# A planned attention and FFN kernel: chunk bounds in another PSUM bank, DMA lateness in the planner, and a refit plan

## The chip, the cores and the metric

The kernel runs on one core of a Trainium2 chip. The metric is device time in microseconds (us) of one execution. The kernel before takes 265.7 us, the median of 13 runs.

## The reference

Four sequences (`B` = 4) of 768 tokens with 8 heads of 64 go through block-sparse causal attention, and its output through a feed-forward network (FFN).

```python
k_min, k_max = k_chunks.min(3), k_chunks.max(3)           # 24 chunks of 32 keys
ub = sum_d(maximum(q * k_min, q * k_max))                 # bound per query and chunk
top_chunks = argsort(where(causal_chunk, ub, -1e9))[..., -6:]
scores = where(in top_chunks and causal, q @ k.T / 8, -1e9)
x = softmax(scores) @ v                                   # [3072, 512]
out = relu(x @ w_in) ** 2 @ w_out                         # 512 -> 2048 -> 512
```

Inputs and output are f32; the kernel computes in bf16 with f32 sums.

## The kernel before

**The work.** A sequence is cut into 6 query tiles of 128. The first tile sees at most four chunks, so its attention needs no selection: it runs densely for all sequences at the start (`first_transposes`, `first_attention`), and the resulting 4 x 128 tokens are the first batch of FFN rows. For the other five tiles the heads go in pairs, 16 in all (`p` = 0 to 15, four to a sequence), in two steps.

`stage_a(p)` prepares a pair. It has the keys and queries with the head dimension on partitions: for sequences 0 and 1 TensorE transposes them into PSUM (`kT`, `qT`); for sequences 2 and 3 (`b >= BY_DMA`, with `BY_DMA` = 2) SP's DMA transposes put them into SBUF (`kt`, `qt`). VectorE then takes chunk maxima and minima (`kr`, L681, two reductions of 0.94 us a pair), spreads them into `kbd`, splits the queries into positive and negative parts (`qp`, `qm`), and copies keys and queries into the operands of the scores (`kqc`, `qsc`). TensorE multiplies to the bounds `ub`, 128 x 240 f32 in PSUM. VectorE adds the causal mask (`ubm`, L706), takes the eight largest of each row (`m`, L655, ten instructions), and compares with the sixth (`selb`). The selection is transposed to `sT`, on TensorE for sequences 0 and 1, by SP's DMA transpose for 2 and 3, and copied into `qsc` as 24 more contraction rows, so that the score matmul itself adds a large negative number to chunks not selected.

`stage_b(p, x)` runs ten banks of scores for a pair (`ps`, L766), ScalarE's exponential (`e`, L788), the causal mask on the diagonal tiles (VectorE L743 or GpSimd L746), the value products (`av`, L777), and VectorE's division into `x` (L594, L596).

`ffn` turns a sequence's `x` into `xT` (TensorE transposes, or SP's DMA transposes for sequences 1 and 2), multiplies by `w_in` (`up`, `ph`, L850), applies ReLU on ScalarE or VectorE (`ht`, L857 and L859), squares on VectorE (`h`, L868), multiplies by `w_out` (`down`, `py`, L881), copies to `ob` and stores a row tile by SP. FFN matmuls are TensorE's filler while VectorE prepares the next pairs.

**The order.** Each operation is recorded with the engines that may do it and a cost on each, a due time, and the tiles it touches. `Plan.order` plays the whole kernel once in the planner's own time. At each step it looks for what can start first, and among the operations of that engine that can start within `wait` of it takes the one with the smallest due time. A load by GpSimd may start only in the order of the string `loads`, then of `later`. The result, sorted by planned start, is written out under a manual schedule, so every engine's instruction order is fixed. `Transfers` is the planner's picture of the DMA engines: it says when a load or transpose ends. Waits on the chip are by semaphores, whatever the planner thought. The numbers in `P` set the due times: `lead` is how far ahead of its scores a pair is prepared, `f_due` places the first tiles, `up_due` and `up_rate` the first FFN batch, `due` and `rate` the other four, `va`, `vm`, `ra`, `h2` the small operations in a pair or FFN step.

**The PSUM banks.** Eight: `tp` 1, `ps` 3, `av` 2, `ff` 2. `kT` and `qT` use `tp`. `ub` and the scores share the three `ps` banks. For sequences 2 and 3 nothing but the DMA transposes takes the place of `kT` and `qT`, so `tp` has no user there.

**The SBUF buffers that the order turns on.** `nt` has 6 for loads that wait for their DMA transpose (the `sT` of sequences 2 and 3 uses the same tag), `kq` 6, `ob` 3, `e` 6.

Of the kernel before, what the change touches and what calls it, by code (L numbers as in the profile page):

```python
# [9 lines left out]
F32 = mybir.dt.float32  # L10
# [31 lines left out]
class Transfers:  # L42
# [10 lines left out]
    def run(self, queues, until):  # L53
        now = self.now
        while now < until and any(queues.values()):
            active = [q for q in queues.values() if q]
            rate = self.RATE / len(active)
            span = min([until - now] + [q[0][1] / rate for q in active])
            now += span
            for q in active:  # L60
                q[0][1] -= span * rate
                if q[0][1] < 1e-6:
                    op = q.pop(0)[0]
                    op.end = now + (0.85 if op.turns else 0.35)
        return until if until < 1e8 else now

    def add(self, op):
# [10 lines left out]
class Plan:  # L78
# [17 lines left out]
        self.ops = []  # L96
        self.loads = []

    def op(self, where, due, fn, needs=(), tiles=(), packets=0, turns=False):
        op = Op(where, due, fn, [n for n in needs if n is not None],  # L100
                [t for t in tiles if t is not None], packets, turns)
        for t in op.tiles:
            t.users.append(op)
        op.number = -1 if packets and not turns else len(self.ops) - len(self.loads)
        self.ops.append(op)
        if packets and not turns:
            self.loads.append(op)
        return op
# [92 lines left out]
def kernel(  # L201
# [11 lines left out]
    B, H, S, D = q.shape  # L213
    CH = 32
    NC = S // CH
# [9 lines left out]
    NP = H // 2  # L225


    NS = NT - 1
    QC = 128 * NS
    VW = 80  # L230
    NSET = 4
    P = dict(lead=[38, 70, 77, 66, 65, 20, 16, 23, 34, 24, 32, 68, 19, 63, 66, 67],
             f_due=[-89, -30, -320.97, -400.97], sp='K0 Q0 K1 Q1', rows=-379,
             rows_after=0, up_due=-1.28, up_rate=3.88, half=4, due=[-6, 1, 3, 45],
             rate=[3.07, 2.84, 4.48, 1.87], va=13.9, vm=5.92, ra=2.68, h2=-1.11,
             later='k1 q1 v1 q2 k2 q3 v3 v2 k3', shift={}, p0=-5650, wait=0.01,
             loads="k0 Q3 K3 q0 Q2 K2 V0 V3 V2 V1 v1 "
                   "k1 i0 v0 i3 q1 i2 v2 k2 i1 q2 o0 q3 k3 o1 o2 v3 o3")

    nc.scalar.preload_act_table_set("natural_log_exp_and_others")  # L240

# [105 lines left out]
    order = []  # L347

    def load(key, fn, due, packets, tiles=(), cost=0.88):
        op = plan.op({"POOL": cost}, due, fn, tiles=tiles, packets=packets)  # L350
        loaded.setdefault(key, []).append(op)

    def first_of(nm, b):
# [12 lines left out]
    BY_DMA = 2  # L366
    turned = {}
    for b in range(B):
        for nm in "kq":
            if b < BY_DMA:  # L370
                nat[nm, b] = buffer("kq", [128, NS, H, D], name=nm + "n")
            else:
                turned[nm, b] = buffer("kq", [128, NT if nm == "k" else NS, NP, 128],
                                       name=nm + "t")

    def turn_by_dma(dst, src, due, needs, tiles, packets=1270):
        return plan.op({"SP": 1.2}, due, lambda _: nc.sync.dma_start_transpose(
            out=dst(), in_=src()), needs, tiles, packets=packets, turns=True)

    raws = {}  # L380

# [33 lines left out]
    def load_turned(nm, b, j, due):  # L415
        dst = turned[nm, b]
        if j == 0:
            src, needs = None, loaded[nm, b, "first"] + loaded[nm, b, 1]
        else:
            src = buffer("nt", [128, H, D])  # L420
            load((nm, b, j), lambda _: nc.gpsimd.dma_start(
                out=src.tile,
                in_=SRC[nm][b, :, 128 * j:128 * (j + 1)].rearrange("h p d -> p h d")),
                due, 1024, [src])
            needs = loaded[nm, b, j]
        i = j if nm == "k" else j - 1
        op = turn_by_dma(
            lambda: dst[:, i],
            lambda: (src.tile if src else firsts[nm][:, b]).rearrange(
                "p h d -> p (h d)"), due, needs, [src, dst])  # L430
        loaded.setdefault((nm, b), []).append(op)

    def load_tile(nm, b, j, due):
# [44 lines left out]
    for what in P["loads"].split():  # L478
        i = int(what[1])
# [10 lines left out]
    for what in P["later"].split():  # L490
        nm, b = what[0], int(what[1])
# [121 lines left out]
    def stage_a(p):  # L613
        b, hp = divmod(p, NP)
# [7 lines left out]
            qT = buffer("tp" if p else "ps", [128, QC], name="qT")  # L622
        kr = buffer("kr", [128, 2, NC])
        qp, qm = buffer("qp", [128, QC]), buffer("qm", [128, QC])
        ub = buffer("ps", [128, NS, 2, NC], F32, name="ub")
        ubm = buffer("ubm", [128, NS, 2, NC], F32)
        m8 = buffer("m8", [128, NS, 2, 8], F32)
        sT = buffer("nt" if b >= BY_DMA else "ps", [128, NT // 2, 128], name="sT")
# [39 lines left out]
        late = 4 if p == 0 else 0  # L668
        if b >= BY_DMA:
            got = list(loaded["k", b])  # L670
            kc_on, qc_on, q_on = {"DVE": 0.36}, {"DVE": 0.40}, 0.39
        else:
            got = [op({"PE": 0.34}, t0, turn_keys, loads_of("k", b, hp) + [made["ident"]],
                      [kT, nat["k", b]])]
            kc_on, qc_on = {"DVE": 0.475, "ACT": 0.74}, {"ACT": 0.63, "DVE": 0.41}
            q_on = 0.40
# [130 lines left out]
    def ffn(x, ready, rows, by_dma, due, rate, up_tags=("ff", "ff")):  # L807
# [12 lines left out]
        def turn(t):  # L820
            if by_dma:
                xt_made.append(turn_by_dma(
                    lambda: xT[:, t], lambda: x[:, t], step(0.225), ready(t),
                    [xT] + xs))
                return
            pt = buffer("ff", [128, NKI, 128], name="xt")

            def go(_):
                for ki in range(NKI):
                    transpose(pt[:, ki], x[:, t, 128 * ki:128 * (ki + 1)])  # L830

# [6 lines left out]
        h2 = {}  # L838

        def up(f, c0, c1, i):  # L840
            tag = up_tags[i % 2]
            w = c1 - c0
            ph = buffer(tag, [128, w], F32, name="ph")
            ht = buffer("ht", [128, w])
            if f not in h2:
                h2[f] = buffer("h2", [128, 128 * n])

            def go(_):
                for ki in range(NKI):
                    nc.tensor.matmul(  # L850
                        ph.tile, lhsT=w_in_sb[:, ki, 128 * f:128 * (f + 1)],
                        rhs=xT[:, c0 // 128:c1 // 128, ki],
                        start=(ki == 0), stop=(ki == NKI - 1))
# [67 lines left out]
    for b in range(B):  # L921
        x = buffer("x", [128, NS, d_model])
        x_done[b, 1] = []
        for p in range(NP * b, NP * (b + 1)):
            stage_a(p)
            stage_b(p, x)
        last = b == B - 1
        turn, up, down = ffn(
            x, lambda t, b=b: x_done[b, 1], [S * b + 128 * t for t in range(1, NT)],
            0 < b < B - 1, HALVES * NP * (b + 1) + P["due"][b], P["rate"][b], ("ps", "ps") if last else ("ff", "ff"))  # L930
        for c in range(2):
            tiles = range(2 * c, 2 + (NS - 2) * c)
            for t in tiles:
                turn(t)
            for f in range(NFI):
                up(f, 128 * tiles[0], 128 * (tiles[-1] + 1), f)
        for t in range(NS - last):
            down(t)
        if last:
            down(NS - 1, 0, 384)  # L940
            down(NS - 1, 384)
# [35 lines left out]
```

## Time and profile before

| What | Value |
|---|---|
| median of 13 runs (lowest to highest) | 265.7 us (264.56 to 266.93) |
| the profiled execution | 265.2 us, span 263.4 us |
| busy: TensorE, VectorE, ScalarE, GpSimd | 252.1, 195.5, 181.8, 104.9 us |
| `ph` and `py` matmuls (L850, L881), busy | 97.1 and 92.5 us |
| DMA: loads by GpSimd's queue | 13.11 MB in 75088 packets |
| median time from issue to landing: `kt`, `qt`, `xT`, `sT` | 3.1 (`kt` from `nt`), 4.8, 2.8, 2.4 us |
| mean granted TensorE clock | 0.994 |

The span runs from the first to the last instruction; 1.8 us of the execution's time lie around it. The slices of the page show the loads filling the DMA engines for about the first half, GpSimd busy with issuing them in the same time, VectorE near full until some 150 us, and TensorE near full from 20 us to the end. Matmuls are pipelined and their ends are modelled, so TensorE's busy share says less than the spacing of its starts.

### The profile page before, as it was taken

What the parts mean: (1) busy time and instruction counts of PE and PEld (TensorE: products, weight loads), DVE (VectorE), ACT (ScalarE), POOL (GpSimd) and SP (SyncE); (2) the same over time, 40 slices, a digit from 0 to 9 for tenths busy, and PEclk for the clock granted to TensorE, in tenths of its full rate; (3) what the DMA queues carried; (4) which work ended last, traced back from release to release, by engine and by line L of the source; (5) the groups of instructions that cost most, each with busy time, mean ns of one, the idle gap of its engine ahead of it and who ended that gap; (6) DMA issues with size and microseconds to landing.
All of it is one profiled execution on the core that took longest, in us unless ns stands there. A gap on an engine that the chain in (4) does not pass through costs nothing.

```text
span 263.4 us, 6518 instructions
## 1 busy us (share of the span) xinstructions
PE 252.1 (96%) x2391; PEld 162.3 (62%) x2391; DVE 195.5 (74%) x687; ACT 181.8 (69%) x372; POOL 104.9 (40%) x182
## 2 busy tenths in 40 slices
PE   7779999999999999998899999999999999999995
PEld 2447655665787665565586665567876548565443
DVE  5699899969998999999999979856777503455000
ACT  1679697973699978795788976688998315276112
POOL 8998868698247697632121221120012000000000
PEclk9799999999999999999999999999999999999999
DMA  9999999999999999983630001335000021100222
GB/s 147 163 181 186 189 181 197 158 121 192 194 83 149 146 144 151 167 124 95 118 97 4 0 2 55 113 82 116 2 0 2 0 80 42 40 5 0 80 80 80
DMA packets 103808, 26.11 MB, mean 99 GB/s; under 512 B 96312, under 2 KB 100832, under 8 KB 103776
## 3 DMA queue, kind: packets, MB, share of 16 engines
q0 software_dynamic: 75088, 13.11, 67.0%
q1 hardware_dynamic: 28688, 12.59, 21.5%
q8 instruction: 18, 0.29, 0.5%
q14 instruction: 14, 0.11, 0.1%
HBM read 27.26 MB, written 6.29 MB: 127 GB/s over the span
## 4 chain that ended last, share of the span: by engine, by line
PE 67%; DVE 20%; ACT 6%; DMA 4%; issue 2%; SPq 1%; DVEq 0%; ACTq 0%
PE ph L850 25%; PE py L881 24%; PE ps L766 8%; DVE kr L681 5%; PE av L777 5%; ACT e L788 2%; DVE m L655 2%; DMA raw<-in_k_dram 2%; DVE h L868 2%; DVE qsc L273 2%; DVE kqc L273 2%; DMA xT<-x 2%; ACT ht L857 1%; ACT qsc L271 1%; DVE qm L697 1%
## 5 line engine op out<-in xcount | busy, mean ns | idle before, releaser
L788 ACT ACTIVATE e<-ps 128x512 bf16<-128x512 f32 x160 | 89.2, 608 | 12.9 <-PE av L777 6.6
L850 PE MATMUL ph<-xT,w_in_sb 128*128 128x256 bf16 (+2 forms) x592 | 97.1, 304 | 0.9 <-DMA xT<-x 0.6
L881 PE MATMUL py<-w_out_sb,h 128*128 128x512 bf16 (+2 forms) x400 | 92.5, 370 | 0.0
L850 PEld LDWEIGHTS <-w_in_sb 128*128 128x128 bf16 x592 | 55.7, 97 | 23.8 <-issue 1.1
L746 POOL TENSOR_SCALAR_AFFINE_SELECT e<-e 128x128 bf16<-128x128 bf16 (+1 forms) x88 | 30.2, 344 | 94.1 <-ACT e L788 90.7
L857 ACT ACTIVATE ht<-ph 128x256 bf16<-128x256 f32 (+2 forms) x121 | 54.6, 455 | 18.0 <-PE ph L850 14.3
L868 DVE TENSOR_TENSOR h<-ht 128x256 bf16<-128x256 bf16 (+2 forms) x148 | 47.2, 328 | 14.6 <-ACT ht L857 10.6
L766 PE MATMUL ps<-qsc,kqc 88*128 88x128 bf16 (+1 forms) x320 | 54.7, 272 | 2.2 <-DVE ubm L706 1.5
L881 PEld LDWEIGHTS <-h 128*128 128x128 bf16 x400 | 35.5, 97 | 31.3
L777 PEld LDWEIGHTS <-e 128*128 128x128 bf16 x640 | 35.1, 97 | 11.8 <-DVE e L743 0.3
L271 ACT COPY ob<-py 128x512 f32<-128x512 f32 (+2 forms) x23 | 13.1, 569 | 35.0 <-PE py L881 34.8
L777 PE MATMUL av<-vn,e 128*128 128x65 bf16 x480 | 35.6, 193 | 0.0
L766 PEld LDWEIGHTS <-kqc 88*128 88x128 bf16 x320 | 26.0, 97 | 12.8 <-issue 3.4
L271 ACT COPY qsc<-sT 24x384 bf16<-24x384 bf16 (+1 forms) x39 | 17.1, 439 | 3.7 <-PE sT L276 2.2
L596 DVE TENSOR_TENSOR x<-av,rc 128x320 bf16<-128x320 f32 (+1 forms) x40 | 18.9, 472 | 0.5
L655 DVE MAX8 m<-ubm 128x8 f32<-128x24 f32 x160 | 15.6, 172 | 0.2
L681 DVE TENSOR_REDUCE kr<-kT 128x24 bf16<-128x768 bf16 x16 | 14.9, 951 | 0.4 <-PE kT L276 0.3
L681 DVE TENSOR_REDUCE kr<-kt 128x24 bf16<-128x768 bf16 x16 | 15.1, 941 | 0.0
L859 DVE TENSOR_SCALAR ht<-ph 128x256 bf16<-128x256 f32 (+2 forms) x27 | 13.0, 486 | 2.4 <-PE ph L850 2.1
L743 DVE TENSOR_TENSOR e<-e,tri 128x128 bf16<-128x128 bf16 (+1 forms) x40 | 9.8, 248 | 6.7 <-ACT e L788 5.9
L777 PE MATMUL av<-v,e 128*128 128x65 bf16 x160 | 14.6, 193 | 0.0
L273 DVE COPY xT<-xt 128x512 bf16<-128x512 bf16 x10 | 4.1, 420 | 12.3 <-PE xt L276 12.3
(85 smaller groups left out, 247.8 us busy)
## 6 DMA issues: line engine op xcount, KB each, us to landing
out_dram<-ob SPq DMA_DIRECT2D x23, 256.0 KB, 2.4
w_in_sb<-in_moe_w_in_dram POOLq DMA_DIRECT2D x4, 512.0 KB, 7.7
w_out_sb<-in_moe_w_out_dram POOLq DMA_DIRECT2D x4, 512.0 KB, 8.0
vn<-in_v_dram POOLq DMA_DIRECT2D x15, 128.0 KB, 6.1
nt<-in_q_dram POOLq DMA_DIRECT2D x10, 128.0 KB, 5.1
nt<-in_k_dram POOLq DMA_DIRECT2D x10, 128.0 KB, 5.0
kn<-in_k_dram POOLq DMA_DIRECT2D x8, 80.0 KB, 6.0
qn<-in_q_dram POOLq DMA_DIRECT2D x8, 80.0 KB, 7.3
```

What stands on the lines that cost most here:

```text
L271: nc.scalar.copy(dst, src)
L596: return plan.op({"DVE": 0.06 + 0.00108 * D * n}, due, lambda _: nc.vector.tensor_mul(x(), av[:, :, 0:D], rc[:, 0:n].unsqueeze(2).to_broad ...
L655: nc.vector.max(out=m8[:, i, hh], in_=ubm[:, i, hh])
L681: nc.vector.tensor_reduce(kr[:, mm].rearrange("d (t c) -> d t c", c=128 // CH) if b >= BY_DMA else kr[:, mm], part(kT).rearrange("d t (c j ...
L746: nc.gpsimd.affine_select(out=e, in_=e, compare_op=ALU.is_ge, fill=0.0, base=0, channel_multiplier=-1, pattern=[[0, n], [1, 128]])
L766: nc.tensor.matmul(ps[:, 128 * c:128 * (c + nt)], lhsT=kqs[:, s, hh, 128 * j:128 * (j + 1)], rhs=qss[:, s, hh, 128 * (t0 - 1):128 * (t0 - ...
L777: nc.tensor.matmul(av[:, t - 1], lhsT=e[:, 128 * c:128 * (c + 1)], rhs=value_tile(b, h, j), start=(i == 0 and c == 0), stop=(i == len(BANK ...
L788: nc.scalar.activation(e.tile, ps.tile, ACT.Exp, scale=scale), [sc], [ps, e])
L850: nc.tensor.matmul(ph.tile, lhsT=w_in_sb[:, ki, 128 * f:128 * (f + 1)], rhs=xT[:, c0 // 128:c1 // 128, ki], start=(ki == 0), stop=(ki == N ...
L857: nc.scalar.activation(ht.tile, ph.tile, ACT.Relu)
L868: {"DVE": 0.067 + w / 1920}, at[0] + P["h2"], lambda _: nc.vector.tensor_mul(h2[f][:, c0:c1], ht.tile, ht.tile), [op], [ht, h2[f]])))
L881: nc.tensor.matmul(py.tile, lhsT=h2[f][:, 128 * t:128 * (t + 1)], rhs=w_out_sb[:, f, c0:c1], start=(f == 0), stop=(f == NFI - 1))
```

## The change

Three things change in the text. The bounds `ub` of sequences 2 and 3 are put into the `tp` bank instead of a `ps` bank. The planner's operations get a lateness, added to the time at which a transfer ends in `Transfers`: 0.5 us for loads, 6.0 us for the transposes of keys and queries, 2.0 us for those of `xT`, none for `sT`; three VectorE costs of sequences 2 and 3 are raised. And nearly all numbers of `P` are others, with another order of loads. No operation is added or taken away; a lateness is no instruction, it moves what the planner lets start after it. The kernel after has five more lines, so its line numbers are up to five higher.

```diff
-                    op.end = now + (0.85 if op.turns else 0.35)
+                    op.end = now + (0.85 if op.turns else 0.35) + op.late
...
-    P = dict(lead=[38, 70, 77, 66, 65, 20, 16, 23, 34, 24, 32, 68, 19, 63, 66, 67],
-             f_due=[-89, -30, -320.97, -400.97], sp='K0 Q0 K1 Q1', rows=-379,
-             rows_after=0, up_due=-1.28, up_rate=3.88, half=4, due=[-6, 1, 3, 45],
-             rate=[3.07, 2.84, 4.48, 1.87], va=13.9, vm=5.92, ra=2.68, h2=-1.11,
-             later='k1 q1 v1 q2 k2 q3 v3 v2 k3', shift={}, p0=-5650, wait=0.01,
-             loads="k0 Q3 K3 q0 Q2 K2 V0 V3 V2 V1 v1 "
-                   "k1 i0 v0 i3 q1 i2 v2 k2 i1 q2 o0 q3 k3 o1 o2 v3 o3")
+    P = dict(lead=[6, 6, 76, 53, 65, 39, 26, 47, 78, 40, 11, 72, 73, 39, 58, 38],
+             f_due=[-36, 144, -224.97, -459.97], sp='K0 Q0 K1 Q1', rows=-639,
+             rows_after=0, up_due=-0.28, up_rate=9.32, half=4, due=[4, -34, -6, 45],
+             rate=[2.94, 3.93, 4.84, 2.12], va=7.79, vm=16.73, ra=0.45, h2=-0.81,
+             later='k1 q1 v1 k2 q2 q3 v2 v3 k3', shift={}, p0=-4820, wait=0.01,
+             loads="q0 K2 V0 k0 Q3 K3 k1 V3 Q2 V2 V1 "
+                   "i0 v1 v0 q1 v2 i2 i3 q2 o0 k2 i1 v3 k3 q3 o3 o1 o2")
...
-        op = plan.op({"POOL": cost}, due, fn, tiles=tiles, packets=packets)
+        op = plan.op({"POOL": cost}, due, fn, tiles=tiles, packets=packets,
+                     late=0.5)
...
-                "p h d -> p (h d)"), due, needs, [src, dst])
+                "p h d -> p (h d)"), due, needs, [src, dst], late=6.0)
...
-        ub = buffer("ps", [128, NS, 2, NC], F32, name="ub")
+        ub = buffer("tp" if b >= BY_DMA else "ps", [128, NS, 2, NC], F32, name="ub")
...
-            kc_on, qc_on, q_on = {"DVE": 0.36}, {"DVE": 0.40}, 0.39
+            kc_on, qc_on, q_on = {"DVE": 0.45}, {"DVE": 0.45}, 0.42
...
-                    [xT] + xs))
+                    [xT] + xs, late=2.0))
...
-            tag = up_tags[i % 2]
+            tag = up_tags[i % len(up_tags)]
```

In `loads` a capital letter with a number is the first tile of a sequence's keys, queries or values; a small `k`, `q` or `v` with a number is that pair of heads of sequence 0, the other five tiles; `i` and `o` are quarters of `w_in` and `w_out`.

More of the change, by code (lines that the diff above doesn't have):

```diff
@@ L97, in __init__, with op @@
         self.loads = []
-    def op(self, where, due, fn, needs=(), tiles=(), packets=0, turns=False):
+    def op(self, where, due, fn, needs=(), tiles=(), packets=0, turns=False,
+           late=0.0):
         op = Op(where, due, fn, [n for n in needs if n is not None],
@@ L103, in op @@
             t.users.append(op)
+        op.late = late
         op.number = -1 if packets and not turns else len(self.ops) - len(self.loads)
@@ L374, with turn_by_dma @@
                                        name=nm + "t")
-    def turn_by_dma(dst, src, due, needs, tiles, packets=1270):
+    def turn_by_dma(dst, src, due, needs, tiles, packets=1270, late=0.0):
         return plan.op({"SP": 1.2}, due, lambda _: nc.sync.dma_start_transpose(
-            out=dst(), in_=src()), needs, tiles, packets=packets, turns=True)
+            out=dst(), in_=src()), needs, tiles, packets=packets, turns=True,
+            late=late)
     raws = {}
@@ L929 @@
             x, lambda t, b=b: x_done[b, 1], [S * b + 128 * t for t in range(1, NT)],
-            0 < b < B - 1, HALVES * NP * (b + 1) + P["due"][b], P["rate"][b], ("ps", "ps") if last else ("ff", "ff"))
+            0 < b < B - 1, HALVES * NP * (b + 1) + P["due"][b], P["rate"][b],
+            ("ps", "ps") if last else ("ff", "ff"))
         for c in range(2):
```

## The prediction

> **What bounds the kernel now.** First the page's busy line, then the table of busy times by stretch, then the waits and the chain inside the stretch that stands out.
>
> ```profile
> PE 252.1 (96%) x2391; PEld 162.3 (62%) x2391; DVE 195.5 (74%) x687; ACT 181.8 (69%) x372; POOL 104.9 (40%) x182
> ```
>
> TensorE looks 96% busy, but that share can't tell full speed from starved. So I count what it streams. In the chain, sixteen 128x512 matmuls take 3.45 us, 0.216 each; four of 384 columns 0.65, so 0.162; four of 256 columns 0.44, so 0.11; transposes stand 0.055 apart, the 65-column value products 0.031. Times their counts in the groups: `ph` 83, `py` 83, `ps` 35, `av` 21, transposes 11, the rest 7: **240 us of streaming in a 263.4 us span**. The other 23 us are what can be won. Setting each matmul's start against the streaming done before it ("lag" = time minus streamed work), I read from the trace: lag 13.0 us at 10 us of work, 13.1 at 25, 14.0 at 35, 14.6 at 50, 15.1 at 60, 15.8 at 80, 17.5 at 110, 19.6 at 130, 19.8 at 190, 20.1 at 240, and 3.2 us from the last matmul to the end. So 13 us go at the start, 2.1 between 10 and 60, **4.5 between 60 and 130**, almost nothing after.
>
> ```profile
> 23.00:38.00 15.00, 14.98 (x145) 9.91 (x145) 13.99 (x53) 11.69 (x24) 11.85 (x15) 1.00 1.65 187
> 38.00:60.00 22.00, 21.64 (x256) 14.28 (x255) 19.81 (x69) 18.53 (x37) 17.60 (x28) 1.00 1.74 163
> 60.00:83.00 23.00, 22.92 (x249) 16.75 (x246) 21.56 (x76) 15.76 (x35) 13.81 (x22) 1.00 1.67 150
> 83.00:125.00 42.00, 40.63 (x411) 25.34 (x410) 41.44 (x144) 34.71 (x70) 25.16 (x44) 1.00 1.66 139
> 125.00:152.00 27.00, 25.93 (x256) 18.42 (x255) 25.99 (x83) 22.77 (x52) 5.89 (x15) 1.00 0.25 53
> 152.00:207.00 55.00, 55.00 (x586) 37.02 (x585) 41.54 (x156) 44.21 (x90) 8.65 (x26) 1.00 0.18 45
> ```
>
> Columns: stretch, length, then PE, PEld, DVE, ACT, POOL busy, clock, DMA. From 83 to 125 us VectorE is busy 41.44 of 42: it is the bound there. From 152 on TensorE is.
>
> ```profile
> PE ps L766 <- DVE ubm L706: 1.5, 3, 0.7
> ACT qsc L271 <- PE sT L276: 1.3, 1, 1.3
> ```
>
> These are waits between 95 and 130 us. The first is the one the bank edit aims at: three score groups waited for a `ps` bank held by chunk bounds that a late VectorE had not read.
>
> ```profile
> 123.00 0.40 DVE x L596
> 123.40 0.86 DVE kr L681
> ...
> 125.56 4.41 DMA xT<-x
> 129.98 0.05 issue
> 130.03 1.06 PE ph L850 x8
> ```
>
> The same stretch's chain: sequence 1's last attention output (123.0), then its DMA transposes, then the FFN matmuls 7.0 us later. TensorE stood 0.74 us at that point.
>
> **The Trainium skill.** "Perfetto Trace Analysis", Identifying the Most-Contended Engine, says that matmul busy share is no measure of distance to the limit; here 40.63 of 42 us busy hides 3 us of lag. "TensorE: Matmul & The Clock Gate", Back-to-back issue gap, gives N/2.4+2.5 ns for an isolated matmul and 131 ns sustained at N=512; the trace shows 216, so the measured spacing is used. "DMA: Bandwidth & Descriptors", Issuing engines are not separate DMA queues, says that DMAs from different engines share the same 16 DMA engines; the trace agrees: `kt` transposes land 2.5 us after issue at 113 to 121 us, `qt` transposes 6.6 us at 93 to 99, beside ten `vn` loads. "PSUM — Partial Sum Buffer", Terms, has one matmul output in one bank; the planner too gives the small `ub` a whole one.
>
> **The change part by part.** The DMA lateness and the refit numbers change the order only. Counting both recorded orders, every VectorE, ScalarE and TensorE operation is there in both; some move between engines (8 selection copies from ACT to DVE, 3 query and 2 `xT` copies the other way, causal masks on DVE 40 to 38, and 20 small warm-up transposes for 2 large warm-up matmuls); the new expression for the tag of `ph` picks the same tag. VectorE's total is 178.4 us in both, by start-to-start spacings where it never waits (kr 0.86, max 0.084, qp and qm 0.395, qsc 0.45 to 0.48, kqc 0.37 or 0.48, x 0.40, h 0.20 to 0.33, and so on). Against its busy time up to 152 us (140.1) that sum (132.7) is low by a factor 1.056, used below. What differs is **how much VectorE work stands ahead of how much TensorE work**:
>
> ```
> PE work us   10    30    50    60    80   100   110   120   130   150
> before     14.7  34.8  51.3  60.9  80.0 101.4 110.8 120.8 131.0 147.6
> after      16.4  35.2  53.0  62.6  82.1 101.8 111.4 118.1 127.3 145.3
> ```
>
> *60 to 130.* Before: 49.9 us x 1.056 = 52.7 for the 50 of TensorE to 110, an excess of 2.7 (the lag grew 2.4); then 20.2 x 1.056 = 21.3 for 20, 1.3 more, plus the 0.74 at `xT`, 2.0 (grew 2.1). The account fits. After: 48.8 x 1.056 = 51.5, an excess of 1.5, and 1.4 if measured to counted stay as before (2.4 to 2.7); then 15.9 x 1.056 = 16.8 for 20: none. The `xT` wait goes: from sequence 1's last output to its first FFN matmul there were 6.6 us of other TensorE work, now 9.5, against the 7.0 that the path took. The bank edit removes the 1.5 us of `ubm` waits, which are inside the excess and not counted again; `tp` is free by then (the last `qT` read in it is at 73 us of work, the first such `ub` after that), and one bank serves, since VectorE reads the bounds one pair after another. What is late next is GpSimd: between 81.6 and 99.2 us of work it gets 17 loads, whose issues stand 0.87 apart in the trace, and 12 masks of about 0.45: 20.2 us for 17.6, so 2.6 late, while the four masks behind the last load have 2.3 to 2.8 us until TensorE uses them. The fourth would be ready 0.8 late; TensorE's own lag gives some of it back. I take 0.6 (0 to 1.5). Sum: lag grows 2.0 in place of 4.5, **gain 2.5** (bounds 0.5 and 3.9).
>
> *Start.* The loads' order puts pair 0's queries first, and more VectorE work before the first FFN matmul: 16.4 against 15.6, 0.8 x 1.056 = 0.9 later if VectorE decides. Landings give a floor: the values of heads 0 and 1 come behind the same set of loads as before (23.66 us) and are now wanted at 10.7 us of work, so lag cannot fall under 13. The added warm-up transposes stand where TensorE waits; if that wait is gone they cost 20 x 0.055 to 0.11, 1 to 2 us less the 2 x 0.216 removed. **Loss 0.6** (0 to 1.7).
>
> *10 to 60.* VectorE owes 1.8 us more by 50. It idled 22 - 19.81 = 2.2 us from 38 to 60, which takes it in; cost 0, and up to 1.3 if dependencies forbid it. Weight chunks come in another order with 0.4 us or more to spare where wanted.
>
> *130 on.* SP issues one `sT` transpose with 2.0 us of work until its first reader, where the least before was 2.4 and the landing takes 2.4: **loss 0.2** (0 to 1). Moved SP work otherwise: the `kt` of sequence 2 go ahead of its `qt` now and have 17 us of work until read, the `qt` 14 or more. These transposes wait on SP for their loads, and output rows queue behind them, one at a time; the three `ob` buffers cover that (cost nothing, 0.5 if two rows met). The tail from 190 us of work is the same stretch of `py` and `ph`.
>
> Sum: -2.5 + 0.6 + 0.2 = -1.7. The profiled execution took 265.2 (span 263.4 and 1.8 around it), so 263.5; the runs' median is 0.5 above the profiled one: **264.0**.
>
> **Rivals.**
> 1. *Slower: the start.* VectorE and ScalarE owe 1.7 and 1.8 us more at 10 us of work. From 23 to 38 us TensorE runs at 14.98 of 15, so a late first FFN matmul is never regained there. If it starts at 24.9 or later, +1.7, and the middle then gains only what the `xT` wait held, 0.7, with GpSimd's 0.6 against it: 265.7 + 1.7 - 0.1 = 267.3. For it: VectorE at 9.5 of 10 from 10 to 20 us. Against: the excess is only 0.9 at the first FFN matmul itself. It decides from a lag of 14.7 at 10 us of work.
> 2. *No difference.* The leveling only moves VectorE's wait; the sum of its work is equal, and it owes 1.7 more at 60; that the bank edit frees a bank which nobody misses belongs here too. Lag 15.8 at 60 and 19.5 at 130: 265.6.
> 3. *More.* VectorE's lateness vanishes, with the start unchanged; only GpSimd's 0.6 is left of the 4.5: 265.7 - 3.9 = 261.8.
>
> **Chances.** A measurement of this kernel can tell about 0.2%, 0.5 us. The forecast 0.60 (own range 262.4 to 265.1), more gain 0.06, no difference 0.14, slower 0.20. So faster by over 0.2% 0.65, within it 0.14, slower 0.21. Range 261.8 to 267.3: it reaches to the first and the third rival's values and leaves out what lies beyond them.
>
> **What would show it.** Right: no `ps` waiting for `ubm` after 95 us; VectorE under 96% busy somewhere between 110 and 130 us of TensorE work; lag near 13.6 at 10, near 17.2 at 110 and at 130; no stand at `xT`. Wrong: a first FFN matmul at 24.9 us or later, a lag at 60 of 16 or more, or waits of `av` for GpSimd's masks after 115 us that add over 1 us.

## The result, and the profile after

The kernel after takes **269.4 us** (median of 11 runs, 267.66 to 270.87): **1.0127 times the kernel before (95% interval 1.0103 to 1.0151), 3.4 us slower**; the kernel before took 265.9 in the 48 runs that this compares it with. One run of 272.02 us, in a slower state of the chip, is left out. The forecast was 264.0 us, a gain of 1.7. The profiled execution took 270.24 us, span 268.5, so 5.1 more span than the profiled one of before. Line numbers are four higher than before around the places in question: `ps` L770, `ubm` L710, `kr` L685, `py` L885, copies L273 (ScalarE) and L275 (VectorE).

The page's busy line, then the busy times by stretch (length, then PE, PEld, DVE, ACT, POOL busy, clock, DMA share and GB/s):

```profile
PE 256.8 (96%) x2409; PEld 165.6 (62%) x2409; DVE 195.4 (73%) x688; ACT 182.2 (68%) x369; POOL 106.3 (40%) x184
```

```profile
23.00:38.00 15.00, 14.54 (x155) 9.87 (x155) 13.15 (x53) 12.30 (x25) 11.48 (x15) 1.00 1.49 171
...
83.00:125.00 42.00, 41.62 (x451) 27.22 (x448) 41.41 (x149) 36.05 (x74) 29.95 (x52) 1.00 1.59 121
125.00:152.00 27.00, 24.84 (x223) 17.11 (x222) 21.17 (x70) 19.03 (x43) 2.89 (x9) 0.94 0.52 93
152.00:207.00 55.00, 54.81 (x566) 36.59 (x566) 44.10 (x161) 44.73 (x90) 10.89 (x29) 1.00 0.18 45
```

From 83 to 125 us TensorE is a full microsecond busier than before, which goes the way of the forecast. The stretch to look at is the next one: 24.84 of 27 us, where before had 25.93, and a clock of 0.94. The waits from 95 to 135 us (sum, times, longest):

```profile
ACT qsc L273 <- DMA sT<-selb: 3.6, 1, 3.6
...
DVE qsc L275 <- DMA sT<-selb: 2.1, 1, 2.1
PE ps L770 <- ACT qsc L273: 2.1, 1, 2.1
```

No score group waits for `ubm` any more. In its place one waits 2.1 us for a copy that waits for the DMA transpose of a selection. TensorE's timeline there (start, duration, what, the wait ahead of it in brackets):

```profile
125.51 1.03 PE L885 MATMUL py<-w_out_sb,h 128*128 128x512 bf16 x4
...
126.40 0.26 PE L781 MATMUL av<-v,e 128*128 128x65 bf16 x3
128.71 0.38 PE L770 MATMUL ps<-qsc,kqc 88*128 88x256 bf16 x2 [2.05 <-ACT qsc L273]
...
131.15 1.91 PE L885 MATMUL py<-w_out_sb,h 128*128 128x512 bf16 x4
...
133.33 1.03 PE L885 MATMUL py<-w_out_sb,h 128*128 128x512 bf16 x4
```

Four 128x512 matmuls take 1.03 us at full speed and 1.91 after the stop: the clock is 0.50 from 129.7 to 133.1 us, which costs another 1.6. The Trainium skill ("TensorE: Matmul & The Clock Gate", What's actually happening) says that TensorE falls to half speed after an idle window of about 3.4 us. Here less was enough. In every profile that has a record of the granted clock (17 of 18), the record changes only on a grid of 3.41 us, which lies differently in each profile. The stop of after lies whole within one cell of the grid, in which TensorE was busy 1.35 us; the next cell ran at 0.50:

```profile
126.30:129.70 3.40, 1.35 (x12) 0.77 (x10) 1.90 (x5) 1.90 (x5) 0.00 (x0) 1.00 0.57 108
129.70:133.10 3.40, 3.40 (x23) 1.78 (x21) 2.77 (x7) 2.46 (x6) 1.29 (x4) 0.50 0.59 153
```

In vec_less (below) a stop as long, 2.09 us ahead of 136.29, lies across the border of two cells at 135.8; TensorE was busy 1.80 us in the first of them, and the clock stayed at 1.00. A stop of 2 us is not always followed by half speed, then, and the 1.6 us are in part luck.

The DMA engines from 119 to 130 us: their rate in GB/s in 40 slices of 0.275 us, then queues and issues with their median landing:

```profile
GB/s 173 305 316 273 188 144 152 150 133 137 149 142 147 155 156 152 172 194 191 171 159 152 210 237 174 78 0 2 8 10 70 288 214 265 118 205 155 1 9 191
...
q8 instruction: 1, 0.02, 0.7%
...
nt<-in_k_dram POOLq DMA_DIRECT2D x3, 128.0 KB, 5.1
xT<-x SPq DMA_TRANSPOSE x5, 4.1
```

The selection of pair 9 was issued at 120.47 us and was there at 127.74, 7.3 us later, in place of about 2.4. Five loads of the last sequence's keys (`nt`) had been issued from 117.11 to 120.60; the last of them landed at 127.88. The engines were busy throughout until 125.9 and moved almost nothing for the next 1.2 us, just behind the start of an instruction fetch (q8) at 125.51.

And the start, after and then before:

```profile
13.78 1.49 PE L278 MATMUL T<-ident,warm 128*128 128x128 bf16 x12
...
17.02 0.21 PE L651 MATMUL ub<-kbd,qp 128*128 128x48 bf16 x1
...
25.55 0.60 PE L854 MATMUL ph<-xT,w_in_sb 128*128 128x256 bf16 x4
```

```profile
14.36 0.18 PE L647 MATMUL ub<-kbd,qp 128*128 128x48 bf16 x1 [0.95 <-ACT e L579]
...
23.23 1.04 PE L850 MATMUL ph<-xT,w_in_sb 128*128 128x256 bf16 x8
```

The first bounds come 2.7 us later, the first FFN matmul 2.3. Lag (time minus streamed work, as in the prediction) by the work done, in the two profiled executions and in that of three kernels below (where a trace lacks records of matmuls, the program's list of them fills in):

```
work us        10    25    40    60    80   105   110   130   140   240
before       13.0  13.1  14.2  15.1  15.8  17.6  17.5  19.6  19.6  20.1
after        15.5  16.6  17.9  18.8  19.6  20.0  23.8  24.7  24.8  25.3
bank_alone   14.3  14.5  15.5  16.4  17.1  18.7  18.6  20.4  20.4  20.8
loads_later  15.1  16.1  17.4  18.4  19.2  19.5  19.5  21.5  21.6  22.1
cut_e        13.5  13.6  14.7  16.4  17.1  17.5  17.5  19.6  20.0  20.5
```

So 5.1 us are: +2.5 up to 10 us of work, +1.2 from 10 to 40, -1.3 from 60 to 105, +2.7 from 105 to 130. One profile misleads at the start: with the same instructions the lag at 10 us came out between 13.0 and 14.3 in eight profiles of the old start (mean 13.65; before's own was the lowest), and between 15.1 and 16.1 in six of the new one (mean 15.6). The start's part is 1.9, not 2.5.

### The profile page after: what moved, and what is told of

It reads as the page before. It is cut to its first block, busy times and chain, and to the rows that moved or that the text cites. A ratio compares the mean times of both kernels' runs of the same rounds, so it can differ in the third digit from the quotient of the medians.

```text
span 268.5 us, 6563 instructions
## 1 busy us (share of the span) xinstructions
PE 256.8 (96%) x2409; PEld 165.6 (62%) x2409; DVE 195.4 (73%) x688; ACT 182.2 (68%) x369; POOL 106.3 (40%) x184
## 4 chain that ended last, share of the span: by engine, by line
PE 65%; DVE 21%; ACT 6%; DMA 4%; issue 2%; SPq 0%; POOL 0%; DVEq 0%; ACTq 0%
PE py L885 25%; PE ph L854 22%; PE ps L770 8%; DVE kr L685 5%; PE av L781 4%; DVE h L872 3%; DVE kqc L275 3%; ACT e L792 2%; DMA xT<-x 2%; DMA raw<-in_k_dram 2%; DVE m L659 2%; DVE qsc L275 2%; ACT qsc L273 2%; DVE x L600 1%; ACT ht L861 1%
## 5 line engine op out<-in xcount | busy, mean ns | idle before, releaser
L792 ACT ACTIVATE e<-ps 128x512 bf16<-128x512 f32 x160 | 89.5, 604 | 16.6 <-PE ps L770 13.6
L885 PE MATMUL py<-w_out_sb,h 128*128 128x512 bf16 (+2 forms) x400 | 93.5, 373 | 0.0
L750 POOL TENSOR_SCALAR_AFFINE_SELECT e<-e 128x128 bf16<-128x128 bf16 (+1 forms) x90 | 32.1, 367 | 97.5 <-ACT e L792 97.5
L770 PE MATMUL ps<-qsc,kqc 88*128 88x128 bf16 (+1 forms) x320 | 58.5, 274 | 2.9 <-ACT qsc L273 2.1
L885 PEld LDWEIGHTS <-h 128*128 128x128 bf16 x400 | 37.1, 98 | 33.5 <-issue 0.7
L781 PEld LDWEIGHTS <-e 128*128 128x128 bf16 x640 | 37.4, 98 | 13.5 <-issue 0.9
L781 PE MATMUL av<-vn,e 128*128 128x65 bf16 x480 | 38.6, 194 | 0.2
L273 ACT COPY ob<-py 128x512 f32<-128x512 f32 (+2 forms) x23 | 13.1, 570 | 34.6 <-PE py L885 34.6
L770 PEld LDWEIGHTS <-kqc 88*128 88x128 bf16 x320 | 24.0, 98 | 10.6 <-issue 4.2
L273 ACT COPY qsc<-sT 24x384 bf16<-24x384 bf16 (+1 forms) x31 | 13.9, 447 | 5.0 <-DMA sT<-selb 4.2
L659 DVE MAX8 m<-ubm 128x8 f32<-128x24 f32 x160 | 15.5, 171 | 0.0
L685 DVE TENSOR_REDUCE kr<-kt 128x24 bf16<-128x768 bf16 x16 | 15.0, 946 | 0.1
L685 DVE TENSOR_REDUCE kr<-kT 128x24 bf16<-128x768 bf16 x16 | 14.8, 948 | 0.1
L747 DVE TENSOR_TENSOR e<-e,tri 128x128 bf16<-128x128 bf16 (+1 forms) x38 | 8.8, 235 | 7.4 <-ACT e L792 6.3
L438 POOL DMA_DIRECT2D vn<-in_v_dram x15 | 13.3, 909 | 0.0
```

Of the source, the lines that this page charges most:

```text
L273: nc.scalar.copy(dst, src)
L659: nc.vector.max(out=m8[:, i, hh], in_=ubm[:, i, hh])
L685: nc.vector.tensor_reduce(kr[:, mm].rearrange("d (t c) -> d t c", c=128 // CH) if b >= BY_DMA else kr[:, mm], part(kT).rearrange("d t (c j ...
L750: nc.gpsimd.affine_select(out=e, in_=e, compare_op=ALU.is_ge, fill=0.0, base=0, channel_multiplier=-1, pattern=[[0, n], [1, 128]])
L770: nc.tensor.matmul(ps[:, 128 * c:128 * (c + nt)], lhsT=kqs[:, s, hh, 128 * j:128 * (j + 1)], rhs=qss[:, s, hh, 128 * (t0 - 1):128 * (t0 - ...
L781: nc.tensor.matmul(av[:, t - 1], lhsT=e[:, 128 * c:128 * (c + 1)], rhs=value_tile(b, h, j), start=(i == 0 and c == 0), stop=(i == len(BANK ...
```

## The experiments

All but one kernel carry their order written out: a list of the planner's operations in place of its search, and nothing else. Their line numbers are 59 higher than after (`ps` L829, `qsc` L332 and L334, `kr` L744). "The first n of one order, then the other" means that the second order's operations follow in their sequence, without those already done. Ratios are to the kernel before, run beside it.

**1. bank_alone.** Before's order, the bank edit only.

```diff
-        ub = buffer("ps", [128, NS, 2, NC], F32, name="ub")
+        ub = buffer("tp" if b >= BY_DMA else "ps", [128, NS, 2, NC], F32, name="ub")
```

> The order of the kernel before, written out, with only the bank of the last two sequences' chunk bounds changed. Theory A (VectorE sets the pace from 83 to 125 us, a score matmul that waits for a bank only shows that VectorE is late): the waits of scores for the bounds' reader go from the trace, the time changes by 0 to -0.6 us against before, 265.5. Rival (the banks themselves hold TensorE): all 1.5 us of those waits come back, 264.4.

265.43 us, ratio 0.9999 (0.9978 to 1.0020). The waits of scores for `ubm` from 95 to 130 us shrank from 1.5 us to one of 0.5 (and `ub` once waited 0.4 for its one bank):

```profile
PE ps L829 <- DVE ubm L769: 0.5, 1, 0.5
```

The time did not move. Here a wait for a bank whose reader was late was VectorE's lateness, seen at another place.

**2. after_no_bank.** After's order, `ub` back in `ps`.

> The order of the kernel after, with the chunk bounds of the last two sequences put back into a ps bank. Theory A (the bank counts for nothing where VectorE or a transpose sets the pace): scores waiting for the bounds' reader come back into the trace, 0.5 to 2 us of them, and the time is within 0.8 us of after, so 1.010 to 1.016 of before. Rival (this order was planned with three ps banks free and needs them): 1.5 to 3 us slower than after, 1.02 of before.

269.66 us, 1.0162 (1.0131 to 1.0192), 0.9 us over after with overlapping intervals. From 95 to 135 us no `ubm` wait came back, and the stop did, shorter:

```profile
128.72 0.38 PE L829 MATMUL ps<-qsc,kqc 88*128 88x256 bf16 x2 [0.89 <-ACT qsc L332]
```

The clock stayed at 1.00 here. One `ubm` wait came back later, where after waits 0.2 us for something else:

```profile
153.54 0.38 PE L829 MATMUL ps<-qsc,kqc 88*128 88x128 bf16 x2 [1.11 <-DVE ubm L769]
```

So in the old order the bank is worth less than can be measured; in the new one it may be worth up to about 0.9 us, which these runs don't settle.

The two profiles also split the stop. Here the selection of pair 9 took 6.3 us (121.45 to 127.75) beside the same five loads, and an instruction fetch began only at 127.39, so the stop of 0.89 is as good as the loads' alone. The other 1.2 us of the stop in after's profile go with its fetch at 125.51, and were not isolated.

**3. loads_later.** After's order, five loads moved.

```
- GpSimd: ... k3 load 1, 2, 3, 4, 5, masks of pair 8, masks of pair 9 (first four) ...
+ GpSimd: ... masks of pair 8, masks of pair 9 (first four), k3 load 1, 2, 3, 4, 5 ...
```

> The kernel after, with the five loads of the last sequence's keys moved behind the fourth diagonal mask of pair 9 on GpSimd, some 13 us later; nothing else moved. Theory A (those loads fill the DMA engines just when the selection of pair 9 is to be transposed): that transpose lands 2.3 to 3.5 us after issue instead of 7.4, no stop of TensorE at 126 us, lag growth from 105 to 115 us of work under 1.5 instead of 4.0, time 1.5 to 3.9 us under after, about 267. Rival C (a fetch of instructions on the DMA engines holds the transpose, loads or not): it still lands over 5 us after issue, time within 0.7 us of after, 269.2.

267.12 us, **1.0080** (1.0048 to 1.0113), 1.3 us less by the ratios than after (the intervals just overlap; vec_less and no_warm below, which share its later loads, lie at 1.0076 and 1.0088). ScalarE's copy of the selection starts 3.7 us after its issue (120.00 to 123.66) and TensorE passes the place without a wait:

```profile
126.03 0.38 PE L829 MATMUL ps<-qsc,kqc 88*128 88x256 bf16 x2
126.25 1.03 PE L944 MATMUL py<-w_out_sb,h 128*128 128x512 bf16 x4
127.11 0.29 PE L840 MATMUL av<-vn,e 128*128 128x65 bf16 x4
```

Lag from 105 to 110 us of work grows 0.03 in place of 3.9. The loads cause this stop. The median gains less than the profile did, for two reasons that the traces show. The stop's size varies: in after_no_bank's profile it cost 1.2. And the five loads now start at 129.35, beside the next pair's selection (issued at 129.34), which lands after 3.52 us where after had 2.33. VectorE waits 1.3 us for it, and TensorE for VectorE:

```profile
DVE qsc L334 <- DMA sT<-selb: 1.3, 1, 1.3
...
134.87 1.03 PE L913 MATMUL ph<-xT,w_in_sb 128*128 128x256 bf16 x8 [1.08 <-DVE ht L922]
```

Eight kernels have the later loads. In seven of them (loads_later, vec_less, no_warm, keys_first, cut_b, cut_c, cut_d) that selection landed 3.4 to 4.3 us after issue and TensorE lost 0.7 to 2.3 us there; in cut_e it went out 0.7 us ahead of the loads, landed after 2.4 and cost nothing. So moving the loads exchanged one such stop for a smaller one, and the difference of 1.3 should understate what the first one cost. The Trainium skill ("DMA: Bandwidth & Descriptors", Queues, rings and completion order) says that a completion count is written only after every earlier write of that DMA engine, of its other queues too. The trace of after fits it, with the selection there at 127.74 and the load issued next to it at 127.88; but engines that are simply full would look the same.

**4. start_before** and **5. start_after.** One order up to the first FFN matmul, the other from there on.

> The kernel after, but everything up to the first FFN matmul stands in the order of the kernel before (loads included); the rest as after. Theory A (the loss has two parts: 2.5 us from the new start, kept to the end, and a stop at 126 us worth 1.4 to 3.9): first FFN matmul near 23.2 us again, lag at 10 us of work near 13.0, time 2.0 to 3.0 us under after, about 266.9. Rival B (TensorE's late start is taken up by VectorE's lateness between 60 and 130 us of work, so only the stop counts): lag at 110 us of work as in after, time within 0.8 us of after, 269.

> The kernel before, but everything up to the first FFN matmul stands in the order of the kernel after; bank of the bounds as before. Theory A (the new start costs by itself and is kept): first FFN matmul near 25.5 us, lag at 10 us of work near 15.5, time 2.0 to 3.0 us over before, 268.4. Rival B (absorbed where VectorE is late): 0 to 0.8 us over before, 266.3.

start_before: 268.59 us, 1.0132 (1.0092 to 1.0172), no gain over after. start_after: 269.74 us, 1.0172 (1.0134 to 1.0209), 4.5 us over before. So neither did what my theory said in numbers. In start_before the lag at 10 us is 13.5, but at 15 us it is 15.0:

```profile
25.23 0.34 PE L840 MATMUL av<-vn,e 128*128 128x65 bf16 x3 [0.85 <-DVE e L806]
```

The first causal masks stand on VectorE behind the reductions of pair 1, which the new order had done ahead of the first FFN matmul and the old start had not. Cutting two orders where they have done different things costs by itself (start_after lost 2.2 from 15 to 20 us of work). The next cuts were put where both had done nearly the same.

**6. cut_a** and **7. cut_b.** The orders exchanged after 400 operations. cut_b has the later loads.

> The reverse: the order of the kernel after for its first 400 operations, then that of before, with the bank of before. Theory A (the new order's first 40 us of work cost 2.5 to 3.7 us, which nothing later takes up): lag at 40 us of work 2.5 to 3.5 us above before, growth from 60 to 130 4 us or more as in before, ratio 1.010 to 1.014, 268.4 us. Rival B (a late TensorE finds VectorE caught up): growth from 60 to 130 only 2 us, ratio 1.002 to 1.006.

> The order of the kernel before for its first 400 operations (some 40 us of TensorE's work; at that place both orders have done the same but for two operations each), then the order of the kernel of the later loads, with its bank. Theory A (the new order's middle is better by itself): lag growth from 60 to 105 us of work 1.1 to 1.4 in place of 2.3, no stop at 126 us, time 0.8 to 1.5 us under before, ratio 0.995. Rival B (the middle grows less only because TensorE comes to it 2.5 to 3 us later, when VectorE has caught up): growth 2.2 or more, ratio 0.999 to 1.004.

cut_a (new start): 268.20 us, 1.0110 (1.0084 to 1.0137), theory A. Its lag at 40 us is 18.0, 3.2 over the mean of before and bank_alone, and from 60 to 130 it grows 4.1, much as in before (4.5) and bank_alone (4.0). **The new start costs about 3 us and nothing later takes it up.** cut_b (new middle): 265.82 us, 1.0010 (0.9993 to 1.0028). Its lag grows 1.2 from 60 to 105 us although TensorE comes there early, so rival B's mechanism is out; but its number came true. 0.5 us went at the cut, 0.7 at the selection beside the later loads, 0.9 at 135 to 140 us.

**8. cut_c, 9. cut_d, 10. cut_e.** The same as cut_b at 460, 433 and 409 operations.

> As the cut at 400 operations, but at 460, where both orders have again done the same but for two operations (some 43 us of TensorE's work). Theory A (0.5 us of the middle's gain were lost at the place of the cut, where lag grew 0.7 in place of 0.2): lag growth from 30 to 60 us of work 1.3 as in before, from 60 to 105 1.2, time 0.5 to 1.2 us under before, ratio 0.996 to 0.998. Rival (what the middle gains is lost again later, at the selections of pairs 11 and 12): ratio 0.999 to 1.002.

> The cut at 433 operations, the place where both orders have done the same but for one score group and one load: before's order up to there, then that of the later loads. Theory A: the middle's gain is kept whole, lag growth from 30 to 60 us of work 1.3 as in before and from 60 to 105 1.2, time 0.5 to 1.2 us under before, ratio 0.9955 to 0.998. Rival: lag is lost again behind 105 us, in the stretch of the selections by DMA, as it was in the two cuts before: ratio 0.999 to 1.003.

> The same at 409 operations, where the two orders differ by one FFN matmul group and one score group. Theory A: as at 433, ratio 0.9955 to 0.998. Rival: 0.999 to 1.003. The two cuts should agree within 0.5 us, unless the transposes by DMA of one of them meet a fetch of instructions on the DMA engines, which shows as a landing of 3.5 us or more with no load beside it.

cut_c 267.11 us, 1.0070 (1.0042 to 1.0097); cut_d 266.02, 1.0016 (0.9996 to 1.0037); cut_e 265.65, 1.0007 (0.9983 to 1.0031). Growth from 60 to 105 us of work is 1.2 in all three, against 2.1 to 2.5 with the old middle. In cut_d and cut_e 0.9 goes between 45 and 50 us of work (before 0.25), in cut_c 1.9: pair-preparing VectorE work of the new middle is wanted there, and `kT` waits for its one bank. In cut_c:

```profile
61.89 0.22 PE L337 MATMUL kT<-ident,k 128*128 128x128 bf16 x1 [0.53 <-DVE kr L744]
```

The other loss (0.4 to 0.9 at 135 to 140) is one selection that landed 3.8 to 4.2 us after issue with no load beside it. Between these two places, cut_c and cut_d lose 1.2 to 1.3 at the selection beside the later loads; cut_e doesn't, and loses 1.3 at 146.85, where ScalarE waits 1.2 us for the selection after that. No version here beats the kernel before.

**11. no_warm.** loads_later without the twenty small warm-up transposes.

> The kernel of the later loads, without the twenty small warm-up transposes (1, 3 and 1 groups of four). Theory A (twelve of them stand 1.28 us ahead of the first chunk bounds in TensorE's queue, and VectorE waits 1.7 us for those): the first bounds 0.9 to 1.3 us sooner, first FFN matmul near 24.2 us, time 0.7 to 1.2 us under that kernel, 1.004 of before. Rival (they only fill a time in which TensorE waits anyway, or they keep its clock up): no gain, or 0.3 to 1 us slower, 1.008 to 1.012.

267.73 us, 1.0088 (1.0059 to 1.0117): no gain, so the rival. Two 128x512 presets in loads_later, then the same two in no_warm:

```profile
19.48 0.59 PE L617 MATMUL ps<-ahead,ident 128*128 128x512 bf16 x2
```

```profile
18.92 1.06 PE L617 MATMUL ps<-ahead,ident 128*128 128x512 bf16 x2
```

The lag at 10 us splits into warm-up matmuls, matmuls spaced at half speed, and gaps: 4.0 + 2.4 + 7.6 in loads_later, 2.1 + 4.7 + 6.8 in no_warm, 2.7 + 2.5 + 6.7 in before (the rest is the 1.1 us up to the first of them; the border between the last two terms is a choice, and 1 us can pass from one to the other). In these profiles, what the warm-ups cost comes back as half speed when they are left out.

**12. keys_late.** Before, only two pairs of loads exchanged.

```diff
- loads: k0 Q3 K3 q0 Q2 ...
+ loads: q0 Q3 K3 k0 Q2 ...
```

> The kernel before, with only the loads of pair 0's keys and queries exchanged: queries first, keys fourth, as in the kernel after; every engine's other instructions in the same order. Theory A: the first maximum starts near 12.5 us in place of 9.8, the first FFN matmul 1.5 to 3 us later, time 1.5 to 3 us over before, ratio 1.006 to 1.011. Rival D: under 0.5 us later, ratio under 1.002.

267.82 us, **1.0113** (1.0079 to 1.0146), theory A. TensorE waits for the keys, the first `kr` starts at 12.63 us in place of 9.84, the first FFN matmul at 26.00 in place of 23.23 (against the means of the eight old starts, 10.1 and 23.9, both come 2.5 and 2.1 later):

```profile
11.90 0.69 PE L337 MATMUL kT<-ident,kn 128*128 128x128 bf16 x5 [2.81 <-DMA kn<-in_k_dram]
```

**13. keys_first.** loads_later with keys and queries of pair 0 exchanged in loads, transposes and VectorE's queue, and the first bounds moved behind the queries' transposes.

> The kernel of the later loads, with keys and queries of pair 0 changing places at the start: the two loads of the keys first and those of the queries fourth, their TensorE transposes and VectorE's operations on them exchanged, and the first chunk bounds right behind the queries' transposes. Theory A (the start is late because the keys' two loads stand third from last among the first six and the chain from keys to maxima, bounds, selection and scores is the longest): first maximum near 9.5 us in place of 12.5, first FFN matmul 0.9 to 1.8 us sooner than 25.1, time 0.9 to 1.8 us under that kernel, ratio to before 1.001 to 1.0045. Rival D (VectorE's added work or the values' landing decides): first FFN matmul under 0.5 us sooner, ratio 1.006 to 1.010.

270.03 us, 1.0185 (1.0150 to 1.0221): 2.8 us slower than loads_later, where a gain was expected. The first `kr` did start at 10.15 us; the first FFN matmul came at 27.36.

```profile
14.25 0.40 PE L337 MATMUL xt<-ident,x 128*128 128x128 bf16 x4 [1.50 <-DVE x L659]
```

VectorE now did the keys' reductions ahead of the first tile's attention output `x`, and TensorE stood for that. Two chains share VectorE's queue at the start; here moving one alone hurt the other.

**14. vec_less** and **15. vec_less_before.** The reductions of pairs 1 and 2 read a quarter of the keys, in loads_later and in before.

```diff
-                    part(kT).rearrange(... "d (c j) -> d c j", j=CH),
+                    part(kT).rearrange("d (c j) -> d c j", j=CH)[
+                        :, :, 0:CH // 4 if p in (1, 2) else CH],
```

> The kernel of the later loads, in which the chunk maxima and minima of pairs 1 and 2 are taken over the first 8 of each chunk's 32 keys (this part of the computation is changed): four reductions of 0.95 us become four of some 0.3, so VectorE has 1.3 us less to do ahead of the first FFN matmul and 1.3 more before 35 us of TensorE's work. Theory F (the start is late because the new order puts 1.3 to 1.8 us more of VectorE's work ahead of the same TensorE work): lag at 10 us of work down 0.8 to 1.3, at 25 us down 1.5 to 2.5, time 1.5 to 2.5 us under that kernel, ratio to before 0.999 to 1.003. Rival G (landings or TensorE's own queue decide): lag at 10 down under 0.4, time under 0.7 us less, ratio 1.005 or more.

> The same cut of VectorE's work in the order of the kernel before, in which the reductions of pair 1 stand just ahead of the first FFN matmul and those of pair 2 later (this part of the computation is changed). Theory F: the first FFN matmul and lag at 10 us hardly move (under 0.4), since what stands there waits for loads and for scores; lag at 25 to 60 down at most 0.5, where VectorE has idle time; later, where it has none, down 1 to 2; ratio 0.993 to 0.998. Rival G: as the other kernel, under 0.7 us less, ratio 0.998 to 1.000.

vec_less: 267.80 us, 1.0076 (1.0046 to 1.0106), the same as loads_later. VectorE's two reductions of pair 1 there:

```profile
20.25 0.33 DVE L744 TENSOR_REDUCE kr<-kT 128x24 bf16<-128x192 bf16 x1
20.82 0.35 DVE L744 TENSOR_REDUCE kr<-kT 128x24 bf16<-128x192 bf16 x1
```

They cost 0.95 each in loads_later. With 1.2 us less of VectorE work ahead of it, the first FFN matmul still came 12.4 us after the first `kr`, as in loads_later (25.12 - 12.76): theory F falls. (The time alone would not tell, since this profile has a stop of 2.09 us at the selection beside the later loads, where loads_later's has 1.08.) vec_less_before: 264.66 us, 0.9970 (0.9949 to 0.9990), a gain of 0.8 for 2.4 us of work taken away, 0.5 of it between 25 and 30 us of TensorE's work.

**16. late_alone.** Before with only the lateness and the raised costs, its own numbers `P`, planned anew.

> The kernel before with only the planner's lateness and its three raised costs; the numbers P, the order of loads and the bank as before; the planner makes a new order of it. Theory A (lateness by itself only pushes work of the last two sequences' pairs back; gain and loss of the change come from the new numbers P): start as before, first FFN matmul within 0.5 us of 23.2 to 24, time within 1.5 us of before on either side, ratio 0.995 to 1.006. Rival E (the lateness levels VectorE's work): lag growth from 60 to 105 us of work about 1.2, time 1 to 1.5 us under before, ratio 0.995.

272.20 us, **1.0262** (1.0235 to 1.0289). The start is as before (lag 13.6 at 10 us), but lag grows 4.2 from 60 to 105 and 4.2 from 105 to 130, and neither theory foresaw that:

```profile
118.82 0.60 PE L770 MATMUL ps<-qsc,kqc 88*128 88x256 bf16 x4 [1.43 <-ACT qsc L273]
...
135.10 1.03 PE L854 MATMUL ph<-xT,w_in_sb 128*128 128x256 bf16 x8 [1.62 <-ACT ht L861]
```

The lateness is no gain by itself, with numbers that were chosen without it. The new numbers without the lateness were not run.

## Why the prediction was wrong

**What bounded the kernel** was read rightly: VectorE from 83 to 125 us, TensorE's stream from 152 on (growth from 130 us of work to 240: 0.5 before, 0.6 after).

**60 to 130 (forecast -2.5).** In the profile it was +1.4 (growth 5.9 in place of 4.5). Right in kind, from 60 to 105: growth 1.1 to 1.3 in place of 2.1 to 2.5, a gain of 1.2, in every kernel with the new middle. The sum of VectorE's work ahead of TensorE's told that. From 110 to 130 its "none" for VectorE's excess held too: after grew 0.9 where before grew 2.1, no score group waited for `ubm`, nothing stood at `xT`, and VectorE was busy 21.17 of 27 us from 125 to 152 us. (loads_later grew 2.0 there, but 1.2 of it is the second stop, behind a transpose.) The term that failed is "what is late next". It named GpSimd's masks behind its loads, 0.6 us, and left out the landing of the selections, which the prediction takes as 2.4 us elsewhere. GpSimd's loads were the right suspects, but not for their issue time: they filled the DMA engines just when SP's transpose of pair 9's selection was to pass. I had counted instructions on each queue and left out what stands in the DMA engines behind them, though the prediction itself cited that all queues share them and that `qt` transposes landed 6.6 us after issue beside ten loads. The stop cost 3.7 us in the profile of after (2.1, and 1.6 of half speed), 2.7 net of the 1.0 that before lost elsewhere in that stretch and after did not. In the median it is known only as after's 1.3 over loads_later, which has the smaller stop in its place. Pair 9's selection was issued 6.2 us ahead of its reader's place (120.47 to 126.66), so beside a usual landing of 2.4 us nothing looked late.

**130 on (forecast 0.2).** Right within its bounds: growth 0.1 from 130 to 140 us of work in after. The transpose with 2.0 us of slack that was named there cost nothing; the one that cost had three times that slack, and met the loads.

**Start (forecast 0.6, at most 1.7).** It was 1.9. The step took VectorE's sum, 0.9, and the landing of the values as a floor. vec_less shows that VectorE's sum doesn't decide. keys_late shows what does in the old order: two exchanged loads move the first `kr`, and with it the first FFN matmul, by 2.8 us each (2.5 and 2.1 against the means), and the time by 3.0. In all profiles of the old start, keys_late too, that matmul comes 13.4 to 14.4 us after the first `kr`; in those of the new start, keys_first aside, 12.4 to 12.7, with no_warm's 11.8 and after_no_bank's 14.0 outside. The new loads bring the keys fourth (11.70 us against 8.06), `kr` starts 2.8 us later on average (12.9 against 10.1), and the rearranged queues give about 1 us back. That the same holds inside the new order is only argued: keys_first, which should have shown it, met another wait. The warm-ups were priced at 1 to 2 us "if that wait is gone"; they cost 1.3, but stand for half speed that would cost as much.

**10 to 40 (forecast 0, up to 1.3).** 1.15 in after, loads_later, no_warm and cut_a, 1.6 in after_no_bank. "VectorE idled 2.2 us from 38 to 60, which takes it in" came too late: by 25 us of work (38 us in before, 42 in after) 1.0 of the loss had gone, and before that, from 23 to 38 us, VectorE had only 1.0 us idle. Why the work was wanted there was not isolated; vec_less took 2.4 us of reductions away up to there and gained 0.2. The cuts suggest that this early work is the price of the middle's gain: cut_d and cut_e avoid it and pay 0.7 at 45 to 50 instead.

**The bank (forecast nothing of its own)** was right in the old order. In the new one up to 0.9 us stay open.

**Rivals.** The first, slower by the start, had the right place and size (1.7; it decided from a lag of 14.7 at 10 us, and 15.1 to 16.1 came), though its reason, VectorE's and ScalarE's debt, is not what the runs show for VectorE; and it fell short because the stop is in none of the rivals. "Wrong" signs came as named: first FFN matmul after 24.9 us, lag at 60 over 16. Of the "right" signs, those of the middle came (above), those of the lag did not. Sums by the runs: 1.9 + 1.15 - 1.2 + 1.3 of after over loads_later = 3.15; measured 3.4. One reading was off: beside 40.63 of 42 us busy the prediction put 3 us of hidden lag, and by its own measure lag grew 2.4 there.

## What to carry to other kernels

When loads move, list not only when each is issued and wanted, but which small transfers on somebody's path will be in flight beside them; price those by their worst landing in the trace, not by the median. Ask the same again of the place to which a load is moved. At a start, follow the first landing through to the first long matmul, operation by operation, since a sum of one engine's work said little here while the chain waited for one transfer. A part of a plan that is better by itself can be paid for elsewhere: look for where the work that it had done early was done.

## What the runs showed of the hardware that was not expected

Transposes by DMA land later beside a fetch of instructions on the DMA engines. Over 18 profiles, with no loads left (after 144 us), there are 126 transposes of `sT` and `xT`. The 43 with no fetch of 8 or 16 KB from 1.0 us ahead of their issue to 2.6 behind it landed after 2.3 to 2.5 us, median 2.36. The 36 with a fetch of 16 KB that began 0.5 to 2.2 us after issue took 3.1 to 5.1, median 3.98. The other 47 (fetches of 8 KB alone, or at the edges of that window) lie between, 2.3 to 4.4, median 2.52. Stores of result rows ran beside most of them in either group (39 of 43, 30 of 36), so these are not the difference. Fetches of 16 KB come 8 to 18 us apart for most of the kernel, so a transpose with under 2 us to spare meets one now and then, another one in another kernel. The stops of the cuts at 135 to 140 us of work are of this kind.

The second thing is the grid of the granted clock, and where stops lie on it. The cell of 3.41 us with 1.35 us of TensorE work in after was followed by a cell at 0.50; cells with 1.80 in vec_less (132.4 to 135.8), 1.84 in keys_first (135.3 to 138.7) and 1.78 in late_alone (133.4 to 136.8) were not. At the start of no_warm a cell with 2.04 us (15.5 to 18.9) was, so busy time by itself does not settle it, and no run here looked for the rule.
